# A pre-norm block with linear attention and a feed-forward layer: projections, folds and state updates of the first third in another order

## The chip, the cores and the metric

The program runs on one core of one Trainium2 chip. The metric is the device time of one execution in microseconds (us). The core has a matrix engine (TensorE, PE in the rows), a vector engine (VectorE, DVE), an activation engine (ScalarE, ACT), GpSimd (POOL) and SyncE (SP), which here only issues DMAs. Each engine takes its instructions in a fixed order; they wait for each other by semaphores.

## The reference

```python
x = A_x                                     # 1 x 2048 x 640, bf16; H = 32 heads of Dh = 20
# A(layernorm(x)):
qkv = x @ wqkv                              # 640 -> 3 * 640
pq, pk = q @ w_phi[h], k @ w_phi[h]         # 20 x 20 for each head
phi_q = concat([softmax(pq), softmax(-pq)]) # 40 features
phi_k = concat([softmax(pk), softmax(-pk)])
kv = phi_k^T v;  z = sum_s phi_k            # not causal: one state for all tokens
o  = (phi_q kv) / (phi_q z + 1e-6)
h  = x + o @ wo
h2 = h + silu(layernorm(h) @ w1) @ w2       # 640 -> 1728 -> 640
```

## The kernel before

The 2048 tokens are 16 tiles of 128 (T), in four groups of 4 (G, GT). A group's tokens stand transposed in XnT (5 chunks of 128 features by 512 tokens).

- **Start.** `ln1` normalizes tiles: statistics on VectorE (`stats`, `mv`), the power for `rstd` on GpSimd, the scaled `xn` on VectorE. Group 0 is transposed on TensorE (`xT`); groups 1 to 3 are written to DRAM (`xs`) and come back by a transposing DMA (`xT_dma`). The key weights are transposed on TensorE (`wT`), the query weights by a transposing DMA straight from the input (`wTq`). `fold(1, ce)` multiplies the key weights by w_phi, chunk by chunk, into `Wfk`, and `fold(0, ce)` the query weights into `Wfq`; `phb` holds w_phi spread over a block diagonal with `mask5`.
- **Loop over t.** `stageV(t)` projects tile t by wv into one of the `Vps` buffers. `stageK(t)` projects it by Wfk and makes the 40 features: two exponentials on ScalarE (`Ek`), their sums and reciprocals on VectorE (`Sk`), and the product of Ek by them on GpSimd. `stageC(t)` adds phi_k^T v of the tile to `kv`, which stays in PSUM for all 16 tiles; it needs that product. Beside them run the five `fold(0, c)` and, for group 0, the five `q_unit1` (one of five row blocks of Q each: five matmuls of 512 columns and two exponentials into `EqT`).
- **End of the loop.** `kv_state` multiplies kv by a mask into `KVBD`.
- **Behind it.** `stageQ2` is Q for two row blocks or one (`fill` takes the next of a list). `stageD` multiplies EqT by KVBD and divides (VectorE), `stageT` transposes, `stageG` multiplies by wo, adds x and takes the second norm, `stageTH` transposes again. `stageF1` and `stageF2` are the feed-forward layer of one group, with the D, T, G and TH of the next group between them.

Around the change, `manual_schedule(engines=...)` keeps the named engines' instructions in the order in which the code is written; the other engines' order is set by a scheduler. The `mm2` tiles of the first part take two PSUM buffers in turn; behind the loop (`early.close()`) the same banks make four. Pools on the side "right" (`first`) are given back there.

Of the kernel before, what the change touches and what calls it, by code (L numbers as in the profile page):

```python
# [12 lines left out]
SP = mybir.EngineType.SP  # L13

# [6 lines left out]
def kernel(  # L21
# [14 lines left out]
    T = 16  # L36
# [7 lines left out]
    GT = T // G  # L44
    EPS = 1e-5
# [28 lines left out]
    wv = persist.tile([P, C, D], BF16, name="wv")  # L74
# [13 lines left out]
    make_identity(nc, ident[:])  # L88
    nhalf = persist.tile([P, 4], F32, name="nhalf")
# [20 lines left out]
    Vps = [persist.tile([P, H, 21], BF16, name=f"Vp{i}") for i in range(6)]  # L110

    Wfk = persist.tile([P, C, D], BF16, name="Wfk")
# [6 lines left out]
    hntp = ctx.enter_context(tc.tile_pool(name="hntp", bufs=2))  # L119
# [73 lines left out]
    kv = kvps.tile([P, 3, 512], F32, name="kv")  # L193
# [12 lines left out]
    def stageV(t):  # L206
        ps = proj(t, wv)
        nc.scalar.copy(
            Vps[t % 6][:].rearrange("p (a h) c -> p a h c", a=2)[:, :, :, 0:DH],
            ps[:, :, 0:320].rearrange("p a (h f) -> p a h f", f=DH),  # L210
        )

    def stageK(t):
        ps = proj(t, Wfk)
        Ek = work.tile([P, 2, D], BF16, name="Ek")
# [9 lines left out]
        nc.gpsimd.tensor_tensor(Ek3, Ek3, Sk[:].unsqueeze(2).to_broadcast([P, 2 * H, DH]), op=ALU.mult)  # L225
        ek_of[t] = Ek

    def stageC(t):
        seen = set()
        Ek, Vp = ek_of[t], Vps[t % 6]  # L230
        for (s, r, j0, j1, sl) in PIECES:
            b = sl // 24
            nc.tensor.matmul(  # L233
                kv[:, b, (sl % 24) * 21 : (sl % 24 + j1 - j0) * 21],
# [8 lines left out]
    def kv_state():  # L243
        for b in range(3):
            n = 24 if b < 1 else 24
            nc.vector.tensor_tensor(  # L246
                KVBD[:, 24 * b : 24 * b + n, 0:21],
                kv[:, b, 0 : n * 21].rearrange("p (j c) -> p j c", c=21),
                maskS[:, 24 * b : 24 * b + n, :].to_broadcast([P, n, 21]),
                op=ALU.mult,  # L250
            )
# [36 lines left out]
    with tc.manual_schedule(engines={PE, SP}):  # L288
        load_x(0, 1)
        load_x(1, 2)  # L290
        nc.sync.dma_start(wk[:], wqkv_v[:, :, D : 2 * D])
        load_x(2, 4)
        nc.sync.dma_start(wv[:], wqkv_v[:, :, 2 * D : 3 * D])
        for g in range(1, G):
            load_x(4 * g, 4 * g + 4)
        for r in range(C):
            wT(r)
        for t in range(4):
            ln1([t])
            xT(t)  # L300
# [252 lines left out]
```

## Time and profile before

| | |
|---|---|
| median of 4 runs | 310.55 us (309.31 to 311.27) |
| the profiled execution | 310.27 us |
| its span in the trace | 308.1 us |
| first matmul | 9.0 us |
| K of tile 0 | 28.0 us |
| first C, last C | 40.8 us, 106.8 us |
| first D | 114.45 us |
| first F1 | 147.58 us |

In the rows, a time in front is the start from the beginning of the span and the number behind it how long the group of instructions took, both in us; then engine, line and operation, what it writes and reads, and in square brackets how long the engine stood idle ahead of it, and who ended that. PEld is the loading of matmul weights. A matmul's duration contains its way through the array, so that matmuls overlap: how fast they follow each other is read from their starts.

### The profile page before, as it was taken

How to read it: one execution, taken by the hardware profiler on the slowest of the kernel's cores; microseconds unless marked ns; L12 is line 12 of the kernel's file. 1: busy time of each engine (PE TensorE's matmuls, PEld its weight loads, DVE VectorE, ACT ScalarE, POOL GpSimd, SP SyncE). 2: the span in 40 equal slices, each digit the busy share in tenths (PEclk: the TensorE clock that was granted, in tenths of full speed). 3: DMA queues.
4: the chain of work that ended last, by engine and by line, in shares of the span. 5: the costliest groups of instructions: out<-in, count | busy, mean ns of one | idle time of the engine just before them, and what ended most of it. 6: DMA issues, size and time to landing. Idle time of an engine off the chain costs nothing.

```text
span 308.1 us, 4896 instructions
## 1 busy us (share of the span) xinstructions
PE 260.5 (85%) x1972; PEld 168.9 (55%) x1989; DVE 141.6 (46%) x356; ACT 128.8 (42%) x189; POOL 73.3 (24%) x151
## 2 busy tenths in 40 slices
PE   0577588888986378898899999999999999999994
PEld 0455366666654234554455766556675557754672
DVE  2478754455344328855055546444662555310021
ACT  1546055655744116567655221554213552224300
POOL 6531156654544600221011110110110111100000
PEclk9999799999999859999999999999999999999999
DMA  6903898940000000000000011000010000110011
GB/s 190 360 7 102 191 242 200 404 167 3 0 0 2 0 0 0 2 1 2 0 0 2 0 45 43 2 0 2 22 46 21 0 2 0 45 43 0 2 43 44
DMA packets 20966, 17.21 MB, mean 56 GB/s; under 512 B 12304, under 2 KB 19792, under 8 KB 20944
## 3 DMA queue, kind: packets, MB, share of 16 engines
q1 hardware_dynamic: 20288, 16.88, 17.4%
q8 instruction: 15, 0.25, 0.3%
q10 hardware_dynamic: 656, 0.03, 0.1%
q14 instruction: 7, 0.06, 0.1%
HBM read 9.53 MB, written 4.59 MB: 46 GB/s over the span
## 4 chain that ended last, share of the span: by engine, by line
PE 47%; DVE 23%; POOL 12%; ACT 10%; issue 4%; DMA 2%; SPq 0%; ACTq 0%; POOLq 0%; DVEq 0%
PE mm L456 16%; PE mm L442 11%; POOL Ek L225 6%; PE mm L397 6%; PE mm L200 4%; DVE Sk L223 4%; ACT sq L408 3%; PE mm L260 3%; DVE stats L130 3%; ACT Ek L217 3%; DVE u L374 3%; DVE X L403 3%; PE kv L233 3%; DVE o L377 3%; DMA X<-in_A_x_dram 2%
## 5 line engine op out<-in xcount | busy, mean ns | idle before, releaser
L442 PE MATMUL mm<-HnT,w 128*128 128x512 bf16 x270 | 62.5, 379 | 2.5 <-ACT HnT L433 1.9
L456 PE MATMUL mm<-w,shT 128*128 128x320 bf16 x448 | 63.8, 299 | 0.0
L456 PEld LDWEIGHTS <-shT 128*128 128x128 bf16 x448 | 43.0, 98 | 16.2
L225 POOL TENSOR_TENSOR Ek<-Ek,Sk 128x1280 bf16<-128x1280 bf16 x16 | 37.7, 2354 | 34.4 <-DVE Sk L224 27.7
L442 PEld LDWEIGHTS <-w 128*128 128x128 bf16 x280 | 26.7, 98 | 31.6 <-issue 2.1
L446 ACT ACTIVATE shT<-mm 128x1024 bf16<-128x1024 f32 x28 | 28.7, 1024 | 35.8 <-PE mm L442 35.8
L200 PEld LDWEIGHTS <-XnT 128*128 128x128 bf16 x320 | 31.8, 101 | 18.9 <-DMA XnT<-xs 4.9
L223 DVE TENSOR_REDUCE Sk<-Ek 128x64 f32<-128x1280 bf16 x16 | 23.8, 1485 | 34.9 <-ACT Ek L217 34.9
L403 DVE SCALAR_TENSOR_TENSOR X<-mm,X 128x640 bf16<-128x640 f32 x16 | 13.2, 824 | 46.3 <-PE mm L397 46.3
L410 POOL TENSOR_SCALAR hm<-hst 128x1 f32<-128x1 f32 x16 | 3.2, 202 | 129.1 <-DVE X L403 129.1
L200 PE MATMUL mm<-wv,XnT 128*128 128x320 bf16 x160 | 26.4, 319 | 4.8 <-DMA XnT<-xs 4.6
L463 DVE TENSOR_TENSOR ob<-mm,X 128x640 bf16<-128x640 f32 x16 | 13.2, 823 | 37.2 <-PE mm L456 37.1
L217 ACT ACTIVATE Ek<-mm 128x640 bf16<-128x640 f32 x32 | 20.8, 701 | 15.8 <-PE mm L200 15.8
L233 PE MATMUL kv<-Vp,Ek 128*128 128x147 bf16 (+1 forms) x192 | 14.1, 225 | 14.8 <-POOL Ek L225 14.8
L397 PE MATMUL mm<-wo,ot 128*128 128x320 bf16 x160 | 24.4, 299 | 0.5 <-DVE u L374 0.5
L200 PE MATMUL mm<-Wfk,XnT 128*128 128x320 bf16 x160 | 24.6, 301 | 0.0
L408 ACT ACTIVATE sq<-X 128x640 bf16<-128x640 bf16 x16 | 11.8, 737 | 30.2 <-DVE X L403 25.2
L265 ACT ACTIVATE EqT<-mm 128x1024 bf16<-128x1024 f32 (+1 forms) x18 | 14.9, 885 | 20.0 <-PE mm L260 20.0
L233 PEld LDWEIGHTS <-Ek 128*128 128x128 bf16 x192 | 12.6, 100 | 19.4 <-POOL Ek L225 19.4
L260 PE MATMUL mm<-XnT,Wfq 128*128 128x512 bf16 x71 | 19.4, 411 | 3.5 <-DVE KVBD L246 2.0
L433 ACT COPY HnT<-mm 128x640 bf16<-128x640 bf16 x16 | 11.1, 695 | 22.4 <-PE mm L432 22.4
L397 PEld LDWEIGHTS <-ot 128*128 128x128 bf16 x160 | 15.5, 98 | 8.3 <-DVE u L374 0.7
(63 smaller groups left out, 274.4 us busy)
## 6 DMA issues: line engine op xcount, KB each, us to landing
out_dram<-ob SPq DMA_DIRECT2D x16, 160.0 KB, 1.8
w<-in_B_w_dram SPq DMA_DIRECT2D x1, 2160.0 KB, 10.3
w<-in_B_w_dram SPq DMA_DIRECT2D x1, 2080.0 KB, 15.6
X<-in_A_x_dram SPq DMA_DIRECT2D x3, 640.0 KB, 11.2
xs<-xn SPq DMA_DIRECT2D x12, 160.0 KB, 2.2
wk<-in_A_wqkv_dram SPq DMA_DIRECT2D x1, 800.0 KB, 7.3
wv<-in_A_wqkv_dram SPq DMA_DIRECT2D x1, 800.0 KB, 9.3
wo<-in_A_wo_dram SPq DMA_DIRECT2D x1, 800.0 KB, 5.5
```

What stands on the lines that cost most here:

```text
L200: nc.tensor.matmul(ps[:, half, 0:320], xT_of(t)[:, c, :], W[:, c, half * 320 : (half + 1) * 320], start=(c == 0), stop=(c == C - 1),)
L217: nc.scalar.activation(Ek[:, s, :].rearrange("p (a n) -> p a n", a=2), ps[:, :, 0:320], AF.Exp, scale=1.0 - 2.0 * s,)
L223: nc.vector.tensor_reduce(Sk[:], Ek3, axis=AX.X, op=ALU.add)
L225: nc.gpsimd.tensor_tensor(Ek3, Ek3, Sk[:].unsqueeze(2).to_broadcast([P, 2 * H, DH]), op=ALU.mult)
L233: nc.tensor.matmul(kv[:, b, (sl % 24) * 21 : (sl % 24 + j1 - j0) * 21], Ek[:, s, r * P : (r + 1) * P], Vp[:, HLO[r] + j0 : HLO[r] + j1, :] ...
L260: nc.tensor.matmul(ps[:, i, :], Wfq[:, c, r * P : (r + 1) * P], XnT[g][:, c, :], start=(c == 0), stop=(c == C - 1),)
L397: nc.tensor.matmul(ps[:, half, 0:320], ot_of[t][:, c, :], wo[:, c, half * 320 : (half + 1) * 320], start=(c == 0), stop=(c == C - 1),)
L403: nc.vector.scalar_tensor_tensor(out=Xv, in0=ps[:, :, 0:320], scalar=1.0, in1=Xv, op0=ALU.mult, op1=ALU.add, accum_out=st[:, 0:1],)
L408: nc.scalar.activation(sq[:], X[:, t, :], AF.Square, accum_out=st[:, 1:2])
L442: nc.tensor.matmul(ps[:, i, :], w1[:, c, fc * P : (fc + 1) * P], HnT[g][:, c, :], start=(c == 0), stop=(c == C - 1),)
L446: nc.scalar.activation(shT[g][:, 2 * k : 2 * k + 2, :], ps[:], AF.Silu)
L456: nc.tensor.matmul(ps[:, half, 0:320], shT[g][:, fc, i * P : (i + 1) * P], w2[:, fc, half * 320 : (half + 1) * 320], start=(fc == 0), stop ...
```

## The change

What is computed stays. It is done in another order, with other buffers:

1. In the loop, `stageK(t)` now comes first; `stageV(t)` follows for tiles 4 to 15 (0 to 3 are projected ahead of the loop), and `stageC` runs four tiles behind K instead of two. `Ek` has five buffers instead of three and `Vps` seven instead of six.
2. Behind the loop stand C of tiles 12 to 15, and between the last two the Q of group 1, whole; of the list that `fill` takes, group 1 is gone.
3. The start is reordered: wv is loaded ahead of wk, V and wT and fold alternate, GpSimd is scheduled by hand and builds the masks behind the first two tiles' `rstd`, and `wTq` is loaded behind the tokens, ahead of all writes of `xs`.
4. VectorE is scheduled by hand in the loop: `ln1` of tiles 8 to 11 ahead of it, of 12 to 15 in iteration 5.
5. The last tile's product of Ek is split between GpSimd and VectorE. `kv` is three tiles of one PSUM bank each instead of one tile of three.
6. Behind the loop the fills stand at other places between D, T and G, with D(2) and D(3) moved up. wv, Wfk, Vps, Ek lie in `first`, HnT's pool takes its place; a tile `warm` is set to zero and not read.

```diff
-    Vps = [persist.tile([P, H, 21], BF16, name=f"Vp{i}") for i in range(6)]
+    Vps = [first.tile([P, H, 21], BF16, name=f"Vp{i}") for i in range(NV)]   # NV = 7
...
-    kv = kvps.tile([P, 3, 512], F32, name="kv")
+    kv = [kvps.tile([P, 24, 21], F32, name=f"kv{b}") for b in range(3)]
...
-        Ek = work.tile([P, 2, D], BF16, name="Ek")
+        Ek = first.tile([P, 2, D], BF16, name="Ek", bufs=5)
...
-        nc.gpsimd.tensor_tensor(Ek3, Ek3, Sk[:].unsqueeze(2).to_broadcast([P, 2 * H, DH]), op=ALU.mult)
+        n = H if t == T - 1 else 2 * H
+        nc.gpsimd.tensor_tensor(
+            Ek3[:, 0:n], Ek3[:, 0:n], Sk[:, 0:n].unsqueeze(2).to_broadcast([P, n, DH]), op=ALU.mult,
+        )
+        if n == H:
+            nc.vector.tensor_tensor(
+                Ek3[:, n:], Ek3[:, n:], Sk[:, n:].unsqueeze(2).to_broadcast([P, n, DH]), op=ALU.mult,
+            )
...
-        for b in range(3):
+        for b in (1, 0, 2):
             nc.vector.tensor_tensor(
...
-    with tc.manual_schedule(engines={PE, SP}):
+    with tc.manual_schedule(engines={PE, SP, POOL}):
         load_x(0, 1)
         load_x(1, 2)
-        nc.sync.dma_start(wk[:], wqkv_v[:, :, D : 2 * D])
-        load_x(2, 4)
         nc.sync.dma_start(wv[:], wqkv_v[:, :, 2 * D : 3 * D])
+        nc.sync.dma_start(wk[:], wqkv_v[:, :, D : 2 * D])
+        load_x(2, 4)
         for g in range(1, G):
             load_x(4 * g, 4 * g + 4)
+        nc.sync.dma_start_transpose(wTq[:], A_wqkv[:, 0:D])
...
+        masks()
+        xT(0)
+        xT(1)
+        stageV(0)
+        wT(0)
+        stageV(1)
...
+    with tc.manual_schedule(engines={PE, SP, DVE}):
+        ln1([8, 9, 10, 11])
+        xT_dma(2)
         for t in range(T):
             if t in (1, 5):
-                ln1([t + 7, t + 8, t + 9, t + 10])
-                xT_dma(t // 4 + 2)
-                if t == 1:
-                    nc.sync.dma_start_transpose(wTq[:], A_wqkv[:, 0:D])
-                else:
+                if t == 5:
+                    ln1([12, 13, 14, 15])
+                    xT_dma(3)
+                if t == 5:
                     late_loads()
-            if t + 3 < T:
-                stageV(t + 3)
-            if t >= 2:
-                stageC(t - 2)
+            stageK(t)
+            if t >= GT:
+                stageV(t)
+            if t >= 4:
+                stageC(t - 4)
             if t >= 5 and early_q:
                 early_q.pop(0)()
-            stageK(t)
+        stageC(T - 4)
+        stageC(T - 3)
         stageC(T - 2)
-        for f in early_q:
-            f()
+        stageQ(1, [0, 1], mm2())
+        stageQ(1, [2, 3], mm2())
         stageC(T - 1)
+        q_unit1(1, 4)
         kv_state()
...
-        qs = [(g, rs) for g in range(1, G) for rs in ([0, 1], [2, 3], [4])]
+        qs = [(g, rs) for g in range(2, G) for rs in ([0, 1], [2, 3], [4])]
...
-        fill(1)
         stageD(0)
         fill(1)
         stageD(1)
         stageT(0)
+        stageD(2)
         fill(1)
         stageG(0)
         stageT(1)
-        stageD(2)
+        stageD(3)
...
```

TensorE in iteration 6 before (the first and last rows of each stage; Wfk is K, wv is V, kv is C, phb is the fold; a name's last number is its buffer, mm2_689 is V of tile 9, Ek_579 that of tile 4, mm2_721 K of tile 6):

```order
L200 MATMUL mm2_689<-wv_74,XnT_427 128x320
...
L233 LDWEIGHTS Ek_579
L233 MATMUL kv_133<-Vp4_111,Ek_579 128x168
...
L182 MATMUL mm2_713<-phb_104,wTq_80 128x140
...
L200 MATMUL mm2_721<-Wfk_113,XnT_287 128x320
```

and in iteration 7 of the changed kernel (mm2_685 is K of tile 7, mm2_703 V of tile 7, Ek_483 that of tile 3, mm2_735 K of tile 8):

```order
L193 MATMUL mm2_685<-Wfk_105,XnT_379 128x320
...
L193 MATMUL mm2_703<-wv_74,XnT_379 128x320
...
L233 LDWEIGHTS Ek_483
L233 MATMUL kv0_122<-Vp3_101,Ek_483 128x168
...
L175 MATMUL mm2_727<-phb_95,wTq_80 128x140
...
L193 MATMUL mm2_735<-Wfk_105,XnT_416 128x320
```

K has moved ahead of V and C, V is of the same tile, and C reads an Ek that is two tiles older against K.

VectorE between the norms of tiles 8 to 15 and the first sums of the loop, before (the groups' buffers are mv_395 for tiles 8 to 11 and mv_586 for 12 to 15):

```order
L137 TENSOR_SCALAR xn<-X,mv_395,rstd_412 128x640 x4
...
L131 BN_AGGR mv_586<-stats 128x2
L137 TENSOR_SCALAR xn<-X,mv_586,rstd_603 128x640 x4
L223 TENSOR_REDUCE Sk<-Ek 128x64
L224 RECIPROCAL Sk<-Sk 128x64
```

and in the changed kernel (mv_384 for 8 to 11, mv_532 for 12 to 15; between the two pieces stand four more pairs of sums and reciprocals):

```order
L130 TENSOR_SCALAR xn<-X,mv_384,rstd_401 128x640 x4
L216 TENSOR_REDUCE Sk<-Ek 128x64
L217 RECIPROCAL Sk<-Sk 128x64
...
L123 BN_STATS stats<-X 128x6 x2
L124 BN_AGGR mv_532<-stats 128x2
L130 TENSOR_SCALAR xn<-X,mv_532,rstd_549 128x640 x4
```

The norms of tiles 12 to 15 have moved from ahead of the first sums to behind the fifth.

SP's queue before, from the loads on (the tokens' four loads, the writes and transposing loads of groups 1 to 3):

```order
L85 DMA X<-in_A_x_dram 128x2560 x3
L148 DMA xs_130<-xn 128x640 x4
L150 DMA_TRANSPOSE XnT<-xs_130 128x5x512
L148 DMA xs_131<-xn 128x640 x4
L150 DMA_TRANSPOSE XnT<-xs_131 128x5x512
L321 DMA_TRANSPOSE wTq<-in_A_wqkv_dram 128x5x640
```

and in the changed kernel:

```order
L88 DMA X<-in_A_x_dram 128x2560 x3
L314 DMA_TRANSPOSE wTq<-in_A_wqkv_dram 128x5x640
L141 DMA xs_119<-xn 128x640 x4
L143 DMA_TRANSPOSE XnT<-xs_119 128x5x512
L141 DMA xs_120<-xn 128x640 x4
L143 DMA_TRANSPOSE XnT<-xs_120 128x5x512
```

The load of wTq has moved ahead of groups 1 and 2.

More of the change, by code (lines that the diff above doesn't have):

```diff
@@ L13 @@
 SP = mybir.EngineType.SP
+DVE = mybir.EngineType.DVE
+POOL = mybir.EngineType.Pool
 BF16 = mybir.dt.bfloat16
@@ L73 @@
     wk = first.tile([P, C, D], BF16, name="wk")
-    wv = persist.tile([P, C, D], BF16, name="wv")
+    wv = first.tile([P, C, D], BF16, name="wv")
     wo = persist.tile([P, C, D], BF16, name="wo")
@@ L88 @@
     make_identity(nc, ident[:])
+    warm = first.tile([P, 512], BF16, name="warm")
+    nc.vector.memset(warm[:], 0.0)
     nhalf = persist.tile([P, 4], F32, name="nhalf")
@@ L109 @@
     KVBD = persist.tile([P, 72, 22], BF16, name="KVBD")
-    Vps = [persist.tile([P, H, 21], BF16, name=f"Vp{i}") for i in range(6)]
-    Wfk = persist.tile([P, C, D], BF16, name="Wfk")
+    Vps = [first.tile([P, H, 21], BF16, name=f"Vp{i}") for i in range(NV)]
+    Wfk = first.tile([P, C, D], BF16, name="Wfk")
     Wfq = persist.tile([P, C, D], BF16, name="Wfq")
@@ L499 @@
         stageTH(2)
-        fill(1)
         stageTH(3)
```

77 lines of the change are left out of this document (40 added, 37 removed).

## The prediction

> **What bounds the kernel now.** I read the page's parts 1, 2 and 4 first, then the list of who waited for whom, then the same stretches as a table of windows, and last the timeline of single iterations.
>
> ```profile
> span 308.1 us, 4896 instructions
> PE 260.5 (85%) x1972; PEld 168.9 (55%) x1989; DVE 141.6 (46%) x356; ACT 128.8 (42%) x189; POOL 73.3 (24%) x151
> ...
> PE   0577588888986378898899999999999999999994
> ...
> PEclk9999799999999859999999999999999999999999
> DMA  6903898940000000000000011000010000110011
> ...
> PE 47%; DVE 23%; POOL 12%; ACT 10%; issue 4%; DMA 2%; SPq 0%; ACTq 0%; POOLq 0%; DVEq 0%
> ```
>
> TensorE (PE) is the busiest engine, and yet only 47% of the chain that ended last lies on it: 23% is VectorE, 12% GpSimd. Of 40 slices of 7.7 us, those before the fifteenth hold 3 to 8 with one 9, those from the twenty-first to the last but one 9. So the early part is what waits, and there the clock drops twice (slices 5 and 15). The program's own time is 310.27, 2.17 over its span; the median of the four runs is 310.55.
>
> ```profile
> PE kv L233 <- POOL Ek L225: 14.8, 12, 2.7
> ...
> PE mm L200 <- DMA XnT<-xs: 4.6, 1, 4.6
> ```
>
> PE waits longest for GpSimd's product of Ek, inside stageC. By stretch (busy of PE, PEld, DVE, ACT, POOL, then clock):
>
> ```profile
> 28.00:34.10 6.10, 1.52 (x12) 0.88 (x9) 4.30 (x14) 1.99 (x3) 1.55 (x3) 0.98 0.75 145
> 34.10:41.50 7.40, 6.51 (x43) 4.19 (x44) 5.01 (x8) 2.69 (x4) 2.94 (x2) 0.78 0.70 167
> 41.50:75.70 34.20, 29.94 (x289) 21.98 (x287) 16.22 (x16) 19.41 (x29) 18.83 (x8) 1.00 0.67 213
> 75.70:99.10 23.40, 18.87 (x156) 12.40 (x157) 9.09 (x11) 13.31 (x22) 11.77 (x5) 1.00 0.00 1
> 99.10:110.20 11.10, 3.85 (x39) 2.98 (x36) 5.58 (x7) 1.30 (x2) 4.70 (x2) 0.79 0.01 1
> 110.20:114.45 4.25, 4.03 (x10) 1.49 (x12) 0.00 (x0) 0.00 (x0) 0.00 (x0) 0.50 0.00 0
> 114.45:146.00 31.55, 27.37 (x213) 16.72 (x215) 21.80 (x72) 21.14 (x32) 5.43 (x20) 0.98 0.00 1
> ```
>
> PE idles 4.6 of 6.1 us before the transposed tokens of group 1 arrive, 4.3 of 34.2 and 4.5 of 23.4 in the loop, 7.2 of 11.1 in its tail, and then runs 4.25 us at half clock. One iteration shows the cause:
>
> ```profile
> 49.32 0.84 PE L233 MATMUL kv<-Vp,Ek 128*128 128x168 bf16 x12 [1.20 <-POOL Ek L225]
> ...
> 50.02 1.52 PE L200 MATMUL mm<-Wfk,XnT 128*128 128x320 bf16 x10
> ...
> 51.64 1.30 ACT L217 ACTIVATE Ek<-mm 128x640 bf16<-128x640 f32 x2 [2.78 <-PE mm L200]
> ...
> 52.84 0.84 PE L233 MATMUL kv<-Vp,Ek 128*128 128x168 bf16 x12
> ...
> 52.94 0.69 ACT L208 CAST Vp<-mm 128x640 bf16<-128x640 f32 x1
> 53.03 1.49 DVE L223 TENSOR_REDUCE Sk<-Ek 128x64 f32<-128x1280 bf16 x1 [2.77 <-ACT Ek L217]
> ...
> 54.55 0.55 DVE L224 RECIPROCAL Sk<-Sk 128x64 f32<-128x64 f32 x1
> ...
> 55.28 2.35 POOL L225 TENSOR_TENSOR Ek<-Ek,Sk 128x1280 bf16<-128x1280 bf16 x1 [2.49 <-DVE Sk L224]
> ...
> 56.87 1.49 DVE L223 TENSOR_REDUCE Sk<-Ek 128x64 f32<-128x1280 bf16 x1 [1.76 <-ACT Ek L217]
> ...
> 57.69 0.84 PE L233 MATMUL kv<-Vp,Ek 128*128 128x168 bf16 x12 [0.95 <-POOL Ek L225]
> ```
>
> A tile's K begins at 50.02 and its C at 57.69, 7.7 us later, through two exponentials, a reduction, a reciprocal and the product; C stands two tiles behind K, so a pair of iterations can't be shorter than that chain and the C itself, 8.37 us here (49.32 to 57.69), of which the last C waited 0.95.
>
> **The change part by part.** I rebuild the early part in its new order, from the same durations, and keep what follows it.
>
> *Start of the loop.* Ahead of K(0) stand the same instructions in both kernels (25 and 20 transposes, stageV of tiles 0 to 3 and the five folds of Wfk; before had V(3) just ahead of K(0) too), mixed otherwise. The masks move behind the first two statistics on GpSimd, wv is loaded ahead of wk; both loads have the same size, so first V then wk takes what first wk then V took. I cost these at nothing and keep K(0) at 28.00:
>
> ```profile
> 22.83 1.51 DVE L137 TENSOR_SCALAR xn<-X,mv,rstd 128x640 bf16<-128x640 bf16 x4 [1.14 <-POOL rstd L134]
> 23.30 1.82 SPq L148 DMA_DIRECT2D xs<-xn  x4
> ...
> 28.00 1.52 PE L200 MATMUL mm<-Wfk,XnT 128*128 128x320 bf16 x10
> ...
> 28.63 3.21 SPq L150 DMA_TRANSPOSE XnT<-xs  x1
> ...
> 28.91 1.52 DVE L137 TENSOR_SCALAR xn<-X,mv,rstd 128x640 bf16<-128x640 bf16 x4 [1.13 <-POOL rstd L134]
> ...
> 34.12 2.85 PE L200 MATMUL mm<-wv,XnT 128*128 128x320 bf16 x10 [4.60 <-DMA XnT<-xs]
> ...
> wTq<-in_A_wqkv_dram SPq DMA_TRANSPOSE x1, 6.1
> ```
>
> Now K(0) to K(3) follow each other, and each is held by its own two exponentials (1.30, with a little between them 1.4): they end at 28.0 + 4 x 1.4 = 33.6. They fill the 4.6 us wait. K(4) needs the transposed group 1, which was usable at 34.12, 9.8 us after its last xn (22.83 + 1.51). That chain is not lengthened by the order: the same four statistics and xn come first on VectorE. The transposing load of wTq moves from behind group 2 to ahead of group 1's writes on SP's queue; it took 6.1 us to land. By the DMA digits above the loads are done in the second slice, before 15.4 us, the third slice is empty, and the first write is issued at 23.30, so it lies in that empty stretch of 8 us. Hoisting it costs nothing unless it delays the loads ahead of it. I start iteration 4 at 33.6, between 32.5 (K(0) gains from the new order) and 38 (wTq's issue, some 4 us, comes on top).
>
> *Iterations 4 to 15.* With C four tiles behind, the chain of 7.7 us has some 15 us of PE work above it. PE's own work: from the C at 49.32 to the C at 52.84, which did not wait, K, V and C take 3.52. With a fold it is 3.90 (52.84 to 57.69, less the wait of 0.95). With a Q row:
>
> ```profile
> 75.05 0.84 PE L233 MATMUL kv<-Vp,Ek 128*128 128x168 bf16 x12 [0.95 <-POOL Ek L225]
> ...
> 77.03 1.09 ACT L265 ACTIVATE EqT<-q 128x512 bf16<-128x512 f32 x2 [2.20 <-PE q L260]
> ...
> 79.54 0.84 PE L233 MATMUL kv<-Vp,Ek 128*128 128x168 bf16 x12
> ```
>
> 4.49, no wait in it, so 0.97 a Q row. Iteration 4: 3.52; 5 to 9 with folds: 5 x 3.90 = 19.5; 10 to 14 with Q: 5 x 4.49 = 22.45; 15: 3.52. End at 33.6 + 49.0 = 82.6. Other engines per iteration: GpSimd 2.35, VectorE 2.04, ScalarE 1.30 + 0.69 and 1.09 with Q, all under 3.5, so PE bounds. Ek has five buffers, one more than C's lag, and Vp seven; neither is held.
>
> *New waits.* VectorE's order is now fixed: the statistics of tiles 8 to 11 stand ahead of the first reduction. Their xn ended at 30.43 before (28.91 + 1.52), so Ek(0) is done at 30.43 + 2.05 + 2.35 = 34.9, and C(0) asks for it at 33.6 + 2.8 = 36.4. The statistics of 12 to 15 stand between reductions 4 and 5, and their rstd on GpSimd behind five products: five reductions end at 30.4 + 5 x 2.05 = 40.7, the products at 32.5 + 5 x 2.35 = 44.3, statistics and rstd of four tiles some 5.0 after the reductions (4.57 from 24.34 to 28.91, with one statistic taken early: 45.7), xn 1.5 (47.2), reduction and reciprocal 2.05, product 2.35: Ek(5) at 51.7. C(5) asks in iteration 9 at 33.6 + 3.52 + 4 x 3.90 + 2.8 = 55.5. The cover is 3.8 us; without it each us late costs one, as GpSimd (2.35) then catches up against PE (4.49). Group 3's transposes follow xn (47.2) by the same 9.8: 57.0, wanted by K(12) near 66.
>
> *Tail.* C(12) to C(14), 0.70 each (49.32 to 50.02): 84.7. Q(1) rows 0 to 3 move here from behind the loop, 4 x 0.97: 88.6. They hide Ek(15): its K ends at 80.5, the exponentials at 82.0, reduction and reciprocal at 84.1, the product, now half on each of two engines, at 85.3 (half of 2.35). C(15): 89.3, Q row 4: 90.2. The mask product now waits bank by bank:
>
> ```profile
> 108.28 1.86 DVE L246 TENSOR_TENSOR KVBD<-kv,maskS 128x504 bf16<-128x504 f32 x3 [4.06 <-PE kv L233]
> ...
> 114.45 1.50 PE L357 MATMUL mm<-KVBD,EqT 128*128 128x88 bf16 x14
> ...
> 117.96 0.87 PE L357 MATMUL mm<-KVBD,EqT 128*128 128x88 bf16 x14
> ...
> L301 DVE TENSOR_TENSOR phb<-phr,mask 128x800 bf16<-128x800 bf16 x1 | 0.9, 932 | 0.0
> ```
>
> 1.86 for three, 0.62 each; two of them lie behind C(15): with a wait of 0.2 on each side D(0) starts at 90.9 instead of 114.45.
>
> VectorE's half of Ek(15), 128 x 640 with two operands in SBUF, has phb as its nearest row, 128 x 800 in 0.93, so some 0.75. If the halves ran one after the other, Ek(15) would be done at 84.1 + 0.75 + 1.18 = 86.0, still ahead of 88.6.
>
> *From D(0) to the first F1.* Before this took 33.13 (114.45 to 147.58, below). Two of its eight fills have moved ahead, three Q rows or 2.9, and D(0) ran 0.6 longer than the one at 117.96, at the half clock that follows 7 us of near idleness; neither is left. That gives 29.6. It may be less: D(2) and D(3) now stand earlier, but VectorE is busy 21.8 us in the stretch and F1 waits for the last tile's statistics, so I put the lower bound at 26. The upper is 33.13: if VectorE, not PE, sets the pace, taking Q away gains nothing.
>
> ```profile
> 147.58 2.32 PE L442 MATMUL mm<-HnT,w 128*128 128x512 bf16 x10 [1.95 <-ACT HnT L433]
> ```
>
> F1 then starts at 90.9 + 29.6 = 120.5, 27.1 earlier. What follows, 308.1 - 147.58 = 160.5, is unchanged; PE is busy nearly throughout it. Its weights are issued behind group 3's transposes, some 5 us later than before; by the DMA digits they had all landed within the ninth slice, by 69.3, so they are there. The moved buffers (Ek, Vp, Wfk, wv, HnT) reuse memory that is long idle when it changes hands; the memset of warm, which nothing reads, lies in VectorE's wait for the first tokens. Span 281.0, time 283.2, against 310.27 for the profiled run; on the median's scale 0.3 more, which I leave out.
>
> **The rivals.** *The gain in the stages D to F1 doesn't come* (VectorE sets the pace there). For: from 114.45 to 146 VectorE is busy 21.8 us, in a fixed chain; against: PE had 27.4, more. Then 120.5 becomes 124.0, and the time 286.7.
>
> *The start is late* (wTq's transposes ahead of the writes delay tokens or group 1). For: SP spends 3.21 on the issue of group 1's, and wTq is a quarter larger (640 rows against 512), some 4. Against: an empty stretch of 8 us. Iteration 4 at 38: 287.6.
>
> *The loop stays with GpSimd.* If its product and VectorE's reduction and reciprocal can't overlap when both run without pause, a tile costs 2.35 + 1.49 + 0.55 = 4.39, sixteen from 30.4 end at 100.6, and D(0) starts near 103: 295. Against it: the reduction from 56.87 ran beside a product (55.28 to 57.63) and took 1.49, as the one from 53.03 did with GpSimd idle; and the product took 2.35 both times. The Trainium skill ("SBUF — State Buffer", on the shared port pair) has a rule of this kind, that VectorE and GpSimd lock each other out of a port pair for a whole instruction; read as holding for every VectorE operation it gives the 295. It names VectorE operations with two SBUF inputs or in a two-port mode alone, which of the loop's leaves only Ek(15)'s half and the xn; by that reading, with which the two reductions agree, the 283.2 stands. For the two SBUF inputs the trace has no test, and I leave the rival a small chance.
>
> *Slower than before*, by the same place: D(0) would have to start later than 114.45 + 3.5 = 118, since the stretch behind it is shorter by 3.5. From 30.4 and with 2.5 behind the last product that needs 5.3 us a tile, where 2.35 and 2.04 are shown; it decides from there. Something that slows GpSimd's product itself to twice its time would do it; no row shows that.
>
> **How the numbers follow.** The forecast 0.65; no gain in D to F1 0.13; late start 0.12; loop with GpSimd 0.06; slower 0.02; the change without effect, within 0.5% (about what a measurement of this kernel can tell), 0.02. The likeliest gives 283.2. Its own bounds: iteration 4 at 32.5 and D to F1 in 26 give 278.5. Upwards the first two rivals reach 286.7 and 287.6, both together 291.1, of which I take in all but the end, up to 289.5. Faster 0.96, same 0.02, slower 0.02.
>
> **What would show it.** In the changed profile: no PE wait for Ek in stageC above 0.5 us in sum; K(0) to K(3) in one block near 28 to 34; C to C 3.9 with folds and 4.5 with Q; D(0) near 91, with the clock not at 0.5 there; F1 near 120; from F1 to the end 160.5. I am wrong if PE waits at C(4) or C(5), if reductions or Ek products are longer than 1.49 and 2.35, if F1 comes later than 32 us after D(0), or if the first V or K waits for a load.

## The result, and the profile after

The changed kernel takes 280.64 us (median of 11 runs, 279.69 to 281.12) where the kernel before took 310.85 beside it (16 runs, 308.45 to 312.31): a ratio of 0.9027, 95% interval 0.9004 to 0.9050. The profiled execution took 279.94, its span 278.0. One of the four runs of e3 below (286.53 us, at a lower clock) is over 1.5% above the fastest of its kernel and is left out of its ratio.

The page of the changed kernel, the lines that answer to those of before: busy time, the slices of PE and of its clock, the chain that ended last.

```profile
span 278.0 us, 4890 instructions
PE 254.2 (91%) x1971; PEld 167.8 (60%) x1989; DVE 141.7 (51%) x358; ACT 128.5 (46%) x189; POOL 72.5 (26%) x152
...
PE   0869999999998898799999999999999999999993
...
PEclk9997999999999999999999999999999999999998
...
PE 68%; DVE 12%; ACT 10%; POOL 4%; issue 3%; DMA 1%; ACTq 0%; DVEq 0%
```

From the fourth of 40 slices on (20.9 us) PE is at 9 of ten, but for the stretch from the tail to F1 (slices 13 to 17) and the last slice; in the kernel before that began with the twenty-first. Of the two drops of the clock, the one ahead of D(0) is gone. At the start one is left, now in slice 4: it no longer follows a wait for group 1, but stands in the opening, where V(2) takes 2.58 us instead of 1.52. PE's busy time fell by 6.3 us with the same matmuls. On the chain PE went from 47% to 68%, VectorE from 23% to 12%, GpSimd from 12% to 4%.

The stretches of the changed kernel, cut at K(0), iteration 4, C(12), D(0) and the first F1 (length; busy us of PE, PEld, DVE, ACT, POOL; clock, share of DMA, GB/s):

```profile
0.00:26.46 26.46, 15.23 (x115) 10.64 (x116) 15.47 (x46) 12.29 (x19) 11.73 (x52) 0.94 0.74 218
26.46:32.32 5.86, 5.80 (x41) 3.89 (x41) 4.41 (x7) 4.43 (x7) 1.98 (x3) 1.00 0.84 225
32.32:80.10 47.78, 47.60 (x436) 35.68 (x439) 32.18 (x45) 33.88 (x53) 35.53 (x17) 1.00 0.48 152
80.10:89.65 9.55, 8.26 (x76) 5.19 (x75) 4.35 (x6) 5.08 (x7) 1.91 (x1) 1.00 0.01 2
89.65:117.49 27.84, 23.44 (x196) 14.96 (x200) 20.70 (x71) 17.84 (x29) 5.67 (x20) 1.00 0.00 1
117.49:278.00 160.51, 153.90 (x1112) 97.45 (x1121) 64.60 (x186) 54.93 (x77) 15.72 (x60) 1.00 0.05 17
```

In the loop PE stands still 0.2 of 47.8 us. D(0) starts at 89.65 instead of 114.45, 24.8 us earlier, and F1 at 117.49 instead of 147.58, so 5.3 us more come from the stages between. Behind F1 everything takes what it took (160.51 against 160.52).

Single rows of the changed kernel's timeline, C after C in the loop and the products of Ek on GpSimd:

```profile
31.62 11.62 POOL L219 TENSOR_TENSOR Ek<-Ek,Sk 128x1280 bf16<-128x1280 bf16 x5 [3.77 <-DVE Sk L217]
...
35.03 0.83 PE L233 MATMUL kv<-Vp,Ek 128*128 128x168 bf16 x12
...
42.15 0.83 PE L233 MATMUL kv<-Vp,Ek 128*128 128x168 bf16 x12
...
45.87 0.83 PE L233 MATMUL kv<-Vp,Ek 128*128 128x168 bf16 x12
...
48.30 13.92 POOL L219 TENSOR_TENSOR Ek<-Ek,Sk 128x1280 bf16<-128x1280 bf16 x6 [3.71 <-DVE Sk L217]
...
53.30 0.83 PE L233 MATMUL kv<-Vp,Ek 128*128 128x168 bf16 x12
...
61.50 0.84 PE L233 MATMUL kv<-Vp,Ek 128*128 128x168 bf16 x12
...
65.98 0.84 PE L233 MATMUL kv<-Vp,Ek 128*128 128x168 bf16 x12
```

No C carries a bracket with a wait any more. From one to the next it is 3.72 us with a fold and 4.48 with a Q row. Five products run without a pause, 2.32 each; the first is done at 33.94, 1.1 ahead of C(0). The sixth (Ek(5)) starts at 48.30 and is done at 50.62, 2.7 ahead of C(5).

The tail, from Ek(15) to D(0). Rows 0 to 3 of Q(1) stand between the last two C; row 4, at 87.17, stands behind C(15), so Q(1) is not whole between them:

```profile
81.90 0.83 DVE L223 TENSOR_TENSOR Ek<-Ek,Sk 128x640 bf16<-128x640 bf16 x1
81.94 1.91 POOL L219 TENSOR_TENSOR Ek<-Ek,Sk 128x640 bf16<-128x640 bf16 x1 [2.10 <-DVE Sk L217]
...
86.48 0.83 PE L233 MATMUL kv<-Vp,Ek 128*128 128x168 bf16 x12
...
87.12 1.86 DVE L245 TENSOR_TENSOR KVBD<-kv,maskS 128x504 bf16<-128x504 f32 x3 [4.39 <-PE kv L233]
87.17 1.24 PE L257 MATMUL q<-XnT,Wfq 128*128 128x512 bf16 x5
88.51 1.09 ACT L262 ACTIVATE EqT<-q 128x512 bf16<-128x512 f32 x2
89.65 0.87 PE L386 MATMUL mm<-KVBD,EqT 128*128 128x88 bf16 x14 [1.24 <-ACT EqT L262]
```

C(15) does not wait: its Ek is done at 83.85. D(0) waits 1.24 us, and not for KVBD (ready at 88.98) but for the two exponentials of the last Q row, from 88.51. By the code, the PSUM that D writes is the loop's, and is free when they have read it; in e8, where that row stands earlier, D(0) waits for KVBD instead.

### The profile page after: what moved, and what is told of

Same layout as the page of the kernel before. It is cut to its first block, busy times and chain, and to the rows that moved or that the text cites. A ratio compares the mean times of both kernels' runs of the same rounds, so it can differ in the third digit from the quotient of the medians.

```text
span 278.0 us, 4890 instructions
## 1 busy us (share of the span) xinstructions
PE 254.2 (91%) x1971; PEld 167.8 (60%) x1989; DVE 141.7 (51%) x358; ACT 128.5 (46%) x189; POOL 72.5 (26%) x152
## 4 chain that ended last, share of the span: by engine, by line
PE 68%; DVE 12%; ACT 10%; POOL 4%; issue 3%; DMA 1%; ACTq 0%; DVEq 0%
PE mm L485 18%; PE mm L193 17%; PE mm L471 12%; PE mm L426 6%; PE mm L257 4%; PE kv L233 4%; ACT EqT L262 3%; ACT sq L437 3%; DVE u L403 3%; DVE X L432 3%; DVE o L406 2%; POOL hm L447 2%; PE q L257 2%; DVE hn L449 2%; PE mm L417 2%
## 5 line engine op out<-in xcount | busy, mean ns | idle before, releaser
L219 POOL TENSOR_TENSOR Ek<-Ek,Sk 128x1280 bf16<-128x1280 bf16 (+1 forms) x16 | 36.9, 2331 | 17.8 <-DVE Sk L217 17.8
L492 DVE TENSOR_TENSOR ob<-mm,X 128x640 bf16<-128x640 f32 x16 | 13.2, 823 | 37.5 <-PE mm L485 37.5
L193 PE MATMUL mm<-wv,XnT 128*128 128x320 bf16 x160 | 27.3, 323 | 1.0 <-ACT Wfk L184 0.7
L262 ACT ACTIVATE EqT<-mm 128x1024 bf16<-128x1024 f32 (+1 forms) x16 | 13.9, 914 | 13.7 <-PE mm L257 10.6
L257 PE MATMUL mm<-XnT,Wfq 128*128 128x512 bf16 x65 | 15.8, 379 | 1.2 <-ACT EqT L262 0.8
L123 DVE BATCH_NORM_STATS2 stats<-X 128x6 f32<-128x320 bf16 x32 | 13.6, 461 | 5.9 <-DMA X<-in_A_x_dram 5.9
L386 PEld LDWEIGHTS <-EqT 128*128 128x128 bf16 x224 | 13.8, 98 | 4.5 <-issue 2.2
```

Of the source, the lines that this page charges most:

```text
L193: nc.tensor.matmul(ps[:, half, 0:320], xT_of(t)[:, c, :], W[:, c, half * 320 : (half + 1) * 320], start=(c == 0), stop=(c == C - 1),)
L219: nc.gpsimd.tensor_tensor(Ek3[:, 0:n], Ek3[:, 0:n], Sk[:, 0:n].unsqueeze(2).to_broadcast([P, n, DH]), op=ALU.mult,)
L257: nc.tensor.matmul(ps[:, i, :], Wfq[:, c, r * P : (r + 1) * P], XnT[g][:, c, :], start=(c == 0), stop=(c == C - 1),)
L262: nc.scalar.activation(EqT[g][:, s, rs[0] : rs[-1] + 1, :], ps[:, 0 : len(rs), :], AF.Exp, scale=1.0 - 2.0 * s,)
```

## The experiments

The theory, A: each part of the change takes away a wait of its own (the lag and the place of K those for Ek, the place of wTq one for the query weights, Q(1) the idle tail, the new order of the fills waits between D and F1), and a part that is undone brings that wait back, in some cases with a drop of the clock behind it. The rivals: the lag alone does it all; or the parts only hide behind each other, so that one undone costs nothing. All ratios are to the kernel before; the changed kernel has 0.9027.

| run | what differs | median us | ratio, 95% interval |
|---|---|---|---|
| e1_lag2 | changed kernel, lag 2 | 291.95 | 0.9399 (0.9328 to 0.9471) |
| e11_lag3 | changed kernel, lag 3 | 283.94 | 0.9144 (0.9118 to 0.9171) |
| e3_q1back | changed kernel, Q(1) behind kv_state | 283.02 | 0.9119 (0.9051 to 0.9187) |
| e4_wtqback | changed kernel, wTq behind group 2 | 286.56 | 0.9230 (0.9159 to 0.9301) |
| e5_nosplit | changed kernel, Ek(15) unsplit | 279.81 | 0.9051 (0.9024 to 0.9078) |
| e6_splitmix | changed kernel, all Ek in two pieces | 280.00 | 0.9072 (0.9028 to 0.9117) |
| e7_fillorder | changed kernel, old order D to F1 | 286.08 | 0.9244 (0.9209 to 0.9280) |
| e8_improve | changed kernel, C(15) earlier | 282.81 | 0.9130 (0.9098 to 0.9162) |
| e10_opening | changed kernel, old opening | 283.04 | 0.9121 (0.9096 to 0.9146) |
| e2_kfirst | before, K first in the iteration | 297.87 | 0.9612 (0.9547 to 0.9677) |
| e9_lagonly | before, lag 4 | 297.25 | 0.9541 (0.9466 to 0.9616) |
| e12_orderonly | before, new order D to F1 | 308.53 | 0.9954 (0.9921 to 0.9987) |

### How far C must stand behind K: e1_lag2 and e11_lag3

```diff
-            if t >= 4:
-                stageC(t - 4)
+            if t >= 2:          # e11: 3
+                stageC(t - 2)   # e11: t - 3
 ...
-        stageC(T - 4)
-        stageC(T - 3)           # e11: stays
```

e1: 

> The changed kernel with C two tiles behind K again (K still ahead of V and C). Theory A, the place of K ahead of V and C hides the chain, and the lag of four only carries the start of the loop over: between the end of K(t) and C(t) stand V, C, fold, K, V, C, fold, K and V, some 8.8 us of PE work against a chain of some 6.5, so no wait in the steady loop; only C(0) waits (asked near 30.9, Ek(0) done near 34.0), some 3.4 us in all: 284. Rival B, the lag of four is what removes the waits: the loop waits again in nearly every second C as before, some 9 us: 289 or more. Rival C, the lag has no part in it: 280.6.

e11: 

> The changed kernel with C three tiles behind K. With four, C(5) was asked for 2.7 us after its Ek was done and C(0) did not wait; with two, C(0) waited 4.82 and C(5) 2.82. Theory A (cover, one iteration of 3.5 to 3.7 us per tile of lag): the cover of C(5) becomes about -1.0, C(0) waits about 1.5, both under the 2.8 after which the clock dropped: 281.5 to 284. Rival (any wait there feeds on through the reductions and the statistics behind them): 286 or more. Rival (the lag has slack): 280.6.

With two, rows of the timeline of e1 (C(0), what follows it, reduction 3, C(5), the K behind it):

```profile
34.18 1.45 PE L233 MATMUL kv<-Vp,Ek 128*128 128x168 bf16 x12 [4.82 <-POOL Ek L219]
...
35.47 2.83 PE L193 MATMUL mm<-Wfk,XnT 128*128 128x320 bf16 x10
...
39.67 1.49 DVE L216 TENSOR_REDUCE Sk<-Ek 128x64 f32<-128x1280 bf16 x1 [4.19 <-ACT Ek L210]
...
56.00 0.93 PE L233 MATMUL kv<-Vp,Ek 128*128 128x168 bf16 x12 [2.82 <-POOL Ek L219]
...
57.34 2.85 PE L193 MATMUL mm<-Wfk,XnT 128*128 128x320 bf16 x10
```

Only these two C wait; A had the first alone. Later in the loop they follow each other in 3.71 and 4.48 here too. But with lag two K(3) stands behind C(0) on PE: it starts only at 35.47, runs at half clock (2.83 for the 1.52 that it takes otherwise) and hands its tile over late. Reduction 3 finds VectorE idle for 4.19 us, the statistics of tiles 12 to 15 stand behind the reductions, and so Ek(5) comes to C(5) only at 56.00, where the changed kernel has it done at 50.62. D(0) comes 10.4 us later. A had the first wait right, missed the second, and had under a third of the price (3.4 us expected, 11.3 measured).

With three, the one wait is C(0)'s, in PE's timeline of e11:

```profile
34.19 1.45 PE L233 MATMUL kv<-Vp,Ek 128*128 128x168 bf16 x12 [3.39 <-POOL Ek L219]
35.49 2.83 PE L193 MATMUL mm<-Wfk,XnT 128*128 128x320 bf16 x10
```

3.39 us and a slow K behind them cost 3.3 us by the medians (in the profiled execution D(0) comes 4.7 later). C(5) does not wait, as PE now comes to it later. A's time holds, at the upper end of its range, but not its waits: some 1.5 at C(0) and 1.0 at C(5) were expected. So the fourth tile of lag is for the start of the loop alone, where the first reduction stands behind the statistics of tiles 8 to 11.

### What lag and place of K bring alone: e2_kfirst and e9_lagonly

```diff
# e2, in the kernel before
+            stageK(t)
             if t + 3 < T:
                 stageV(t + 3)
...
-            stageK(t)
# e9, in the kernel before (eight Vp and five Ek buffers; wv, Wfk, Vp, Ek and HnT's pool moved as in the change)
-            if t >= 2:
-                stageC(t - 2)
+            if t >= 4:
+                stageC(t - 4)
 ...
+        stageC(T - 4)
+        stageC(T - 3)
         stageC(T - 2)
```

e2: 

> The kernel before with one statement moved: stageK(t) first in the iteration, ahead of stageV(t + 3) and stageC(t - 2); lag 2, buffers, start, tail and fills as before. Theory A (K's place hides the chain): the waits for Ek between 41 and 99 us go, last K some 12 us earlier, tail of 8 us and half clock stay: about 297 to 299. Rival B (it takes the lag of four and five buffers of Ek): waits stay, 306 to 311.

e9: 

> The kernel before with the lag of C behind K raised from two tiles to four and nothing else of the change (eight buffers of Vp and five of Ek, so that the lag fits); V and C still stand ahead of K, wTq is still loaded behind group 2, Q(1) still runs cold behind the loop. Theory A (each of lag, place of K, wTq, opening and Q(1) is worth its own piece): the waits for Ek inside the loop go, the wait for XnT at the start, C(15)'s wait of about 4 us and Q(1) at half clock stay; D(0) near 100 instead of 114.45, so 294 to 299. Rival B (the lag is nearly all of the gain): 286 or less. Rival C (the lag is worth little while K stands last): 303 or more.

Either does the same: between the first C and the tail no C waits for long any more, at lag two with K first as at lag four with K last (K first puts nearly one more iteration between a tile's K and its C). So they can hardly add, though no run has both and nothing else: 12.1 and 13.2 us alone, both within A's ranges. What is left stands in the tail, in PE's timeline of e2 (C(14), C(15), Q(1)):

```profile
91.28 0.85 PE L233 MATMUL kv<-Vp,Ek 128*128 128x168 bf16 x12 [2.28 <-POOL Ek L225]
94.41 1.45 PE L233 MATMUL kv<-Vp,Ek 128*128 128x168 bf16 x12 [2.28 <-POOL Ek L225]
97.81 3.65 PE L260 MATMUL mm<-XnT,Wfq 128*128 128x512 bf16 x10 [1.96 <-DVE KVBD L246]
```

and of e9, C(15) and Q(1):

```profile
94.46 1.45 PE L233 MATMUL kv<-Vp,Ek 128*128 128x168 bf16 x12 [1.41 <-POOL Ek L225]
97.87 4.45 PE L260 MATMUL mm<-XnT,Wfq 128*128 128x512 bf16 x10 [1.96 <-DVE KVBD L246]
```

The last two products, KVBD, and Q(1) at half clock (10 matmuls of Q that take 2.32 otherwise take 3.65 or 4.45). D(0) starts at 101.30 and 102.11. That rules out the rival that the lag is nearly all of it: 17 of the 30 us are elsewhere.

### Q(1) in the tail: e3_q1back

```diff
         stageC(T - 2)
-        stageQ(1, [0, 1], mm2())
-        stageQ(1, [2, 3], mm2())
         stageC(T - 1)
-        q_unit1(1, 4)
         kv_state()
 ...
+        fill(3)                 # the three of group 1
         stageD(0)
```

> The changed kernel with group 1's Q moved back behind the mask product (three fills ahead of the first D, nothing between the last C's). Theory: they hid Ek(15)'s chain and the mask product; now PE waits some 2 us for Ek(15) and 2 us for the mask product: 283.5 to 285, up to 287 if the clock drops to half behind these waits. Rival, the hiding is worth nothing since D to F1 is held by VectorE: 280.6 to 281.5.

PE's timeline of e3, C(15), the Q fills and D(0):

```profile
83.09 0.84 PE L233 MATMUL kv<-Vp,Ek 128*128 128x168 bf16 x12 [1.59 <-POOL Ek L219]
85.66 7.26 PE L257 MATMUL mm<-XnT,Wfq 128*128 128x512 bf16 x25 [1.72 <-DVE KVBD L245]
92.75 0.87 PE L383 MATMUL mm<-KVBD,EqT 128*128 128x88 bf16 x14
```

C(15) waits 1.59 for its Ek and Q(1) 1.72 for KVBD, close to the 2 and 2 expected. D(0) comes 3.1 later than in the changed kernel, from D(0) to F1 it is 27.95 against 27.84, and the time is 0.9% of the time before longer, just under A's range; the intervals of the two ratios only just part (0.9051 against 0.9050). (Its K(0) started at 24.69, 1.8 earlier; C(0) then waited 0.37 instead of not at all, and at C(11) it was 0.8 ahead.)

### wTq's place: e4_wtqback

```diff
-        nc.sync.dma_start_transpose(wTq[:], A_wqkv[:, 0:D])
         ln1([0])
 ...
         xT_dma(2)
+        nc.sync.dma_start_transpose(wTq[:], A_wqkv[:, 0:D])
         for t in range(T):
```

> The changed kernel with the transposing load of wTq back behind group 2's. Theory: the load was hidden ahead, and here it is not: group 2's issue ends near 35.5, wTq lands 6 us later, near 41.6, and the first fold asks near 39.1: 2.5 us slower, 283. Rival D: hoisting it cost something (its issue took 11.2 us of SP in the changed kernel), so that moving it back frees the start: 279 to 280. Rival E: no difference, 280.6, if the fold's wait is absorbed.

PE's timeline of e4, the first fold of the query weights and the K behind it:

```profile
43.47 0.78 PE L175 MATMUL mm<-phb,wTq 128*128 128x140 bf16 x6 [4.70 <-DMA wTq<-in_A_wqkv_dram]
44.04 2.87 PE L193 MATMUL mm<-Wfk,XnT 128*128 128x320 bf16 x10
```

The first fold waits 4.70 and the clock drops behind it. 2.0% of the time hang on one line's place in SP's queue, over twice what was expected.

### The last product and the two engines: e5_nosplit and e6_splitmix

```diff
# e5
-        n = H if t == T - 1 else 2 * H
+        n = 2 * H
# e6, the second half of every tile
-            nc.vector.tensor_tensor(
+            (nc.vector if t % 2 else nc.gpsimd).tensor_tensor(
                 Ek3[:, n:], Ek3[:, n:], ...
```

e5: 

> The last tile's Ek product whole on GpSimd, as for the other tiles. In the changed kernel its two halves were done at 83.85 us and C(15) was asked for at 86.48. One whole product starting at 81.9 takes 2.32, so it ends at 84.3, still 2.2 us before C(15). Theory A (the split lies beside other work): no change, 279.8 to 281.5. Rival (the split carried the tail): C(15) waits and the time is 282 or more.

e6: 

> Every Ek product is written as two instructions of 640 elements. On even tiles both are on GpSimd, on odd tiles the first is on GpSimd and the second on VectorE. Theory A (the two engines hold each other up when VectorE reads two operands from SBUF): GpSimd's 640 elements take about 1.2 us alone (half of 2.32) and 1.9 us when VectorE's half (0.83) runs beside it, so the slower size is the sum of the two. Rival (half a product simply costs 1.9 on GpSimd): 1.9 on even tiles also, and a whole tile 3.8, slower than the iteration of 3.52, so C would begin to wait. Time by A: 279.5 to 281.5; by the rival 283 or more.

Both are the changed kernel's time, their intervals overlap with its own: the split of Ek(15) brings nothing. (In e6, whose K(0) starts at 24.68, C(0) waits 0.40 and C(5) 0.93 for Ek, and D(0) starts at 89.65 as in the changed kernel.) What e6 shows is the contention. An odd tile and an even tile of its timeline:

```profile
51.28 0.82 DVE L222 TENSOR_TENSOR Ek<-Ek,Sk 128x640 bf16<-128x640 bf16 x1
...
51.32 1.91 POOL L219 TENSOR_TENSOR Ek<-Ek,Sk 128x640 bf16<-128x640 bf16 x1 [3.68 <-DVE Sk L217]
...
54.23 1.27 POOL L219 TENSOR_TENSOR Ek<-Ek,Sk 128x640 bf16<-128x640 bf16 x1 [1.00 <-DVE Sk L217]
...
55.45 1.27 POOL L222 TENSOR_TENSOR Ek<-Ek,Sk 128x640 bf16<-128x640 bf16 x1
```

GpSimd takes 1.27 for 640 elements beside a reduction on VectorE and 1.91 when VectorE's product of two SBUF operands (0.82) starts with it, so most of the 0.82 is added. In other odd tiles VectorE's product starts while GpSimd still works on the tile before, and takes 1.28 to 1.70 itself. The Trainium skill ("SBUF — State Buffer", "Who interferes with whom") has the pair of ports that the two engines share as an exclusive lock; for this form of instruction the trace agrees. For the reduction of the loop it does not bind: five of them take 1.43 to 1.49 beside products of 2.32 in the changed kernel.

### From D to F1: e7_fillorder and e12_orderonly

The six fills of group 2 and 3 stand behind D(0), D(2), D(3), T(2), T(3) and D(4) in the new order, behind D(0), T(0), D(2), D(3), G(2) and TH(1) in the old one.

```diff
# e7, in the changed kernel, down to G(1); the rest as before too
         stageT(0)
-        stageD(2)
         fill(1)
         stageG(0)
         stageT(1)
-        stageD(3)
+        stageD(2)
         fill(1)
         stageG(1)
# e12, in the kernel before, the same place; further down the fills move as in the change
         stageT(0)
         fill(1)
+        stageD(2)
+        fill(1)
         stageG(0)
         stageT(1)
-        stageD(2)
+        stageD(3)
```

e7: 

> The changed kernel with the old order of D, T, G and the fills between D(0) and F1 (six fills left, each where it stood before, without the one ahead of D(0)); the rest stays. D to F1 took 27.84 us in the changed kernel, 33.13 in the kernel before, of which the three Q(1) instructions groups that left are 4.8 to 5.4. Theory A (the gain there beyond Q(1) is small and the order gave about none of it): 280.5 to 281.5. Rival (moving D(2) and D(3) ahead of the fills took waits away): 282 to 284.

e12: 

> The kernel before with the new order of D, T, G and the fills between D(0) and F1 and nothing else: all nine fills of Q stay, one ahead of D(0), eight between (behind D(0), T(0), D(2), D(3), T(2), T(3), D(4) and TH(2)). D(0) to F1 took 33.13 us before with eight fills in the old order, 33.0 with six in the old order and 27.84 with six in the new. Theory A (in the new order PE sets the pace, so two more fills, three Q rows, cost their 3.2 us and D(0) at half clock 0.6): 31 to 31.7, so 308.5 to 309.5, where taking fills away and the new order each give little alone and 5.3 together. Rival B (the order is worth its 5.2 us by itself): about 28, so 305 to 306. Rival C (the order is worth nothing with all the fills): 310 to 311.

Old order with six fills, the waits in PE's timeline of e7 (T(2), the last TH, F1):

```profile
103.94 0.28 PE L417 MATMUL mm<-ident,o 128*128 128x128 bf16 x2 [1.78 <-DVE o L406]
105.19 0.41 PE L417 MATMUL mm<-ident,o 128*128 128x128 bf16 x3 [0.97 <-DVE o L406]
...
121.49 0.45 PE L461 MATMUL mm<-ident,hn 128*128 128x128 bf16 x5 [2.51 <-DVE hn L449]
122.73 3.61 PE L471 MATMUL mm<-HnT,w 128*128 128x512 bf16 x9 [0.78 <-ACT HnT L462]
```

New order with eight fills, PE's timeline of e12, D(0) and the first F1:

```profile
113.63 0.87 PE L357 MATMUL mm<-KVBD,EqT 128*128 128x88 bf16 x14
...
143.75 4.01 PE L442 MATMUL mm<-HnT,w 128*128 128x512 bf16 x10 [2.02 <-ACT HnT L433]
```

From D(0) to F1:

| | old order | new order |
|---|---|---|
| eight fills | 33.13 (before) | 30.12 (e12) |
| six fills | 33.00 (e7) | 27.84 (after) |

In the old order the two fills cost nothing: without them PE is busy 25.04 us instead of 27.37, and stands still 8.0 instead of 5.8. It waits for VectorE, 1.78 and 0.97 at T(2), where the fill behind D(2) is now a single row (1.24 instead of 2.32), and 2.51 at the last TH, ahead of which no fill is left. In the new order they cost 2.3. The order itself is worth 3.0 with the fills in place and 5.2 without them. Part of these sizes is the clock: in the kernel before, D(0) ran 0.6 longer at half clock, which e12's did not, and in e7 a D and a fill behind the waits at T(2) ran 1.6 longer; with these taken off, the order is worth 2.4 and 3.6, and the two fills 1.1 in the old order.

e7's 286.08 lies above the rival's range too. A had put 4.8 to 5.4 on the rows that left, which is all five of Q(1); only three of them stood between D(0) and F1. By itself in the kernel before the order gives 1.9 us, 308.53, at the edge of A's range. Its stage is 0.9 shorter than A's 31, but F1 then starts at half clock (4.01 for ten matmuls, 2.32 in the changed kernel) after a wait of 2.02.

### The opening: e10_opening

```diff
-        nc.sync.dma_start(wv[:], ...)
         nc.sync.dma_start(wk[:], ...)
         load_x(2, 4)
+        nc.sync.dma_start(wv[:], ...)
 ...
+        masks()                     # then wT(0..4), ln1 and xT of tiles 0 to 3,
 ...                                 # and V(0), V(1), folds, V(2), V(3) behind group 1's writes
```

> The changed kernel with the old opening: wk loaded ahead of wv, the mask work first on GpSimd, all transposes, then V, folds of Wfk, V ahead of K(0); wTq still ahead of group 1. K(0) started at 28.00 in the kernel before and at 26.46, 24.88, 24.69 and 24.97 in four runs with the new opening. Theory A (the opening only moves K(0), and K(4) is held in part by the transposed group 1, near 31 to 32): 281.5 to 283. Rival (all of the opening is hidden behind group 1): 280.6. Rival (a later C(0) and a later group 1 feed on as with the lag of two): 286 or more.

PE waits 8.4 us for wk ahead of its first matmul, K(0) starts at 28.87, and D(0) starts at 92.02, 2.37 later than in the changed kernel; from there to F1 it is 27.85 against 27.84. A holds, at the upper end of its range (283.04 for 283): the opening is worth 0.9% and feeds on to nothing.

### A version that was to beat both: e8_improve

```diff
         stageC(T - 2)
-        stageQ(1, [0, 1], mm2())
-        stageQ(1, [2, 3], mm2())
+        q_unit1(1, 4)
+        stageQ(1, [0, 1], mm2())
         stageC(T - 1)
-        q_unit1(1, 4)
```

(Q(1) rows 2 and 3 become the fourth of seven fills, the seventh stands behind TH(2).)

> An attempt to beat the changed kernel. Tail: C(12) to C(14), q row 4 of group 1, Q(1) rows 0 and 1, C(15), kv_state; then D(0) to F1 with the fills Q2 01, Q2 23, Q2 4, Q1 23, Q3 01, Q3 23, Q3 4 in this order, where D(2) and D(3) stand ahead of fills as now. The exponentials that D(0) waited 1.24 us for are done earlier, C(15) can start at about 84.4 when its product is done, and KVBD 2.5 us behind: D(0) at 87.0 instead of 89.65, with a wait of about 1 us, while Q(1) rows 2 and 3 (about 2.0 us) run later, where they take the place of waits of 0.8 to 1.0. Theory A: 278.5 to 280. Rival (the rows moved back cost their 2.0 us and the wait of D(0) for KVBD stays): 280.5 to 282.

PE's timeline of e8, D(0) and the first F1:

```profile
88.08 0.86 PE L385 MATMUL mm<-KVBD,EqT 128*128 128x88 bf16 x14 [1.81 <-DVE KVBD L245]
...
118.66 4.00 PE L470 MATMUL mm<-HnT,w 128*128 128x512 bf16 x10 [2.03 <-ACT HnT L461]
```

D(0) starts 1.6 us earlier, 1.1 less than expected because it waits 1.81 for KVBD; from there to F1 it is 30.58, 2.7 longer, for 2.2 of PE's work; and the exponentials of the last fills stand ahead of the copy that F1 needs, so F1 waits 2.03 and starts at half clock. The rival had the direction right (both of its costs come), though 282.81 lies above its range, and no run is faster than the changed kernel beyond the spread.

## Why the prediction was right, step by step

The profiled execution came out 3.3 us under the 283.2 and the median 2.6, inside the range, and in the loop for the reason given: C no longer waits for Ek, and PE works through. By the prediction's own steps, profiled execution against it:

| step | predicted | measured | difference |
|---|---|---|---|
| to iteration 4 | 33.6 | 32.32 | -1.3 |
| iterations 4 to 15 | 49.0 | 47.78 | -1.2 |
| C(12) to D(0) | 8.3 | 9.55 | +1.25 |
| D(0) to F1 | 29.6 | 27.84 | -1.8 |
| F1 to the end | 160.5 | 160.51 | 0 |
| outside the span | 2.17 | 1.94 | -0.2 |

- **The start of the loop.** "I cost these at nothing and keep K(0) at 28.00" was the wrong step: the same instructions in another mix start K(0) at 26.46, and undoing the mix costs 0.9% (e10). V(0) runs at 8.84, while wk is still on its way, where the old opening waits 8.4 us for wk. With the new opening K(0) differs from run to run: 26.46 to 26.64 where V(2) ran at half clock (here, e5, e7 and e8), 24.68 to 24.97 where it did not (e1, e3, e4, e6 and e11). Little of the earlier start is kept: e6 reaches C(5) at 53.29 and e3 at 52.48, against 53.30 here.
- **The iterations.** 4.48 with a Q row was foreseen at 4.49. With a fold it is 3.72, foreseen at 3.90, and without either 3.40 (35.03 to the next C at 38.43), foreseen at 3.52: both durations were read between two C of the kernel before, and hold 0.1 to 0.2 us that no bracket there explains.
- **The covers** came where they were placed, but smaller: 1.1 instead of 1.5 at C(0), 2.7 instead of 3.8 at C(5). That they are the right places, e1 shows (both waits come back) and e11 for C(0); that "each us late costs one" is too low, e1 shows too.
- **wTq.** The prediction put its issue at some 4 us and its landing at 6.1, in an empty stretch. It was hidden, but not like that. SP's rows in the timeline of the changed kernel, its issue and the first write of xs:

```profile
5.79 11.21 SPq L314 DMA_TRANSPOSE wTq<-in_A_wqkv_dram  x1
...
22.26 1.94 SPq L141 DMA_DIRECT2D xs<-xn  x4
```

From issue to landing it took 13.3. SP was busy with the issue until 17.0, 5.3 us ahead of the first write of xs. With the statistics 5 us earlier the hoist would by these rows have cost time; no run tries that. Nor did the prediction say what the old place would have cost, 2.0% (e4): its sum assumed the weights in time.

- **The tail.** The step that failed is D(0)'s start: the sum had it wait for KVBD alone, 0.7 behind the last Q row. It waited for that row's exponentials instead, 1.4 behind it. And a Q row took 1.08 in the blocks of two (82.17 to 86.48 for four), foreseen at 0.97.
- **From D(0) to F1** the size was nearly right and the step behind it wrong. The 29.6 came from three Q rows that leave (2.9) and the half clock (0.6), the order was given nothing but the lower bound of 26. e7 shows that the rows that leave give 0.1 in the old order: the bound "if VectorE, not PE, sets the pace, taking Q away gains nothing" was right for it. The gain is the order's, and the rows' only with it; that the 29.6 came so near is luck.
- **The other rivals.** The loop did not stay with GpSimd, since reduction and product do overlap; the half of Ek(15), which the prediction said the trace had no test for, did collide (GpSimd's half takes 1.91 beside VectorE's 0.83; both are done at 83.85, ahead of C(15)), hidden as foreseen. The late start did not come.

Whether the parts add up was not foreseen. Undone one at a time they cost 3.7% (lag 2), 2.2% (order), 2.0% (wTq), 0.9% (Q(1)) and 0.9% (opening), together 9.7%, as much as the whole gain; in e2 and e9, put into the kernel before alone, lag and place of K each give 4 to 5% because they remove the same waits. That sum is not proof that nothing overlaps: K first was not undone in the changed kernel.

## What to carry to other kernels

When the busiest engine waits for a chain of other engines, count the chain's length in that engine's own work and put that much between producer and consumer; then look at the first use, where the chain starts late, since a stall there can cost more than itself (at lag three 3.39 us cost 3.3, at lag two 4.82 and what followed from it 11). Filler work taken out of a stage gains only if the work that waits for other engines is spread at the same time: read which wait ends last there before crediting it. Before a DMA is hoisted, look up what its queue's issue takes among the loads it joins, not where it stood.

## What the runs showed of the hardware

- **The issue of a transposing DMA** of the same 640 x 640 weights took 11.21 us on SP and landed after 13.3 behind the queued loads at the start of the program (11.28 and 13.4 in e10); 4.03 and 6.1 behind group 2's in the kernel before, 3.88 and 7.4 in e4. Why was not tried apart.
- **The length of a wait does not tell whether the clock halves.** It dropped behind single waits of 4.82, 4.70, 3.39 and 2.82 us, and in e8 and e12 behind 2.03 and 2.02 (ten matmuls of F1 in 4.00 and 4.01 us). It did not behind 2.74 at C(14) in the kernel before (C in 0.85, the granted clock 1.00 in the 1.6 us behind the wait), nor behind 2.48 at C(0) in e2, 1.95 at F1 in the kernel before (2.32), or 1.59 and 1.72 in e3. And in the opening V(2) ran at half clock behind waits of 1.10 and 0.75 in the changed kernel, but at full clock behind 1.10 and 0.74 in e3 (1.52). C(0) of e2 and V(2) of the changed kernel, in PE's timelines:

```profile
40.96 0.85 PE L233 MATMUL kv<-Vp,Ek 128*128 128x168 bf16 x12 [2.48 <-POOL Ek L225]
...
20.20 2.58 PE L193 MATMUL mm<-wv,XnT 128*128 128x320 bf16 x10 [0.75 <-ACT Wfk L184]
```

The Trainium skill ("TensorE: Matmul & The Clock Gate", "What's actually happening") has the slow state after at least one idle window of about 3.4 us; here it also came behind waits of 2.0 to 2.8, and behind shorter ones. What separates those that halved it from those that did not stays open.
